# A Fourier mixing layer with a SoLU feed-forward behind it: where GpSimd's projection sums stand, and how the last two pairs are handled

## The chip, the cores and the metric

The kernel runs on one core of one Trainium2 chip. The core has five engines with an instruction queue each: TensorE (PE, matmuls; its weight loads are shown apart as PEld), VectorE (DVE), ScalarE (ACT), GpSimd (POOL) and SyncE (SP), which here issues transfers only. Each engine works through its own queue in order, and an instruction that waits holds up everything behind it on that engine. The metric is device time in microseconds (us).

## The reference

Eight sequences of 3136 tokens with 256 channels go through a Fourier filter, and every token then through a feed-forward block with a SoLU and a layer norm:

```
X = np.fft.rfft(x, axis=1)
y = np.fft.irfft(X * (filt_r + 1j * filt_i), n=3136, axis=1)
h = y.reshape(25088, 256) @ w_in                      # 1024 hidden
e = np.exp(h - h_max)
solu = h * e / (np.sum(e, axis=-1, keepdims=True) + 1e-09)
ln = (solu - mu) / np.sqrt(var + 1e-06) * g_ln
out = ln @ w_out                                      # 256 channels
```

## The kernel before

The 25088 tokens form 196 blocks of 128, and two blocks form a pair (98 pairs). One step of the main loop belongs to one block; there are 205 steps, written out by hand in `step(k)`, so the order of each engine's queue is the order of the calls there. `j` is `k // 2`. Both matrix products use a seven-product scheme for 2 x 2 blocks (as in Strassen's), so each needs sums of input blocks beforehand.

The way of a pair `q`, whose blocks are 2q and 2q+1:

- Steps 2q and 2q+1: `pair_sums` (four small sums s on GpSimd, one step ahead), seven `product` calls on TensorE, and `keep` and `finish` on ScalarE and VectorE, which give h and its running maximum.
- Two steps later for each block: `exponential` (ScalarE, into the single buffer e) and `normalize` (VectorE, L771). Three steps later: `turn` (a transpose of 32 x 32 blocks, VectorE, L787) and `square` (ScalarE, L779, which gives the variance).
- Two pairs make a group `g` of four blocks, which share one turned tile and one row of variances. Once the last block of the group is turned, `regroup` (eight transfers from SP, L799) puts a pair's tokens in order into two tiles solu_t: at step 2q+6. For the first pair of a group, `deviations` (GpSimd, L806 and L808, called rs below) computes the reciprocal deviations, SP writes them out as rows (L810), and `regroup_deviations` reads them back as rs_t (four transfers, L816).
- `project_sums(q, 0)` in odd step 2q+7 makes the sum u1 and the difference written over a part of solu_t; `project_sums(q, 1)` in even step 2q+8 makes u2 and u4. All four are GpSimd sums of 128 x 512 elements, and all are recorded under the helper's line L702. u2 and u4 have one buffer each, so a pair's u4 waits for the projection of the pair before that read it.
- Steps 2q+9 and 2q+10: seven `project` calls of four matmuls each (L844), in the order 1, 2, 6, 7, then 5, 3, 4. Products 1, 6, 5, 3 use one PSUM bank, and ScalarE's `keep_out` (L856, scaled by rs_t) must read it between any two of them. Products 2, 7, 4 use a second bank, read by `finish_out` on VectorE (L860). `store_out` writes the result from SP (L868).

The Fourier filter of sequence 2 to 8 runs along with this, at the steps that a hand-made plan gives: x rows are fetched, GpSimd makes a sum x (L260, in `products[k]`) and VectorE a difference, TensorE makes the first stage pa (L269), ScalarE evacuates it, GpSimd stores it (L280); a spectrum stage follows (pb, pc, g; filter rows f loaded by GpSimd, L642; g stored by GpSimd, L343), and the way back (rows t loaded by GpSimd, L356; py, join on VectorE). So GpSimd's queue holds sums, and issues of transfers, of both halves of the kernel. The plan ends before step 166; after that only the work on tokens is left. After step 195 nothing but the last blocks and projections remains (the tail, steps 196 to 204). Pool "r" holds four buffers of [128, 4, 256] for x and t rows; nothing uses them in the tail.

Of the kernel before, what the change touches and what calls it, by code (L numbers as in the profile page):

```python
# [9 lines left out]
FP32 = mybir.dt.float32  # L10
I32 = mybir.dt.int32
AFT = mybir.ActivationFunctionType
ALU = mybir.AluOpType
# [4 lines left out]
P = 128  # L18
B, S, C = 8, 3136, 256
DFF = 1024  # L20
# [9 lines left out]
NCH = 4  # L30
KD, KF = C // P, DFF // P
# [63 lines left out]
def kernel(  # L95
# [10 lines left out]
    nc = tc.nc  # L106
# [295 lines left out]
    with ExitStack() as st:  # L402
        fpool = pool("fp", 1, stack=st)
        pools = {name: pool(name + "0", bufs, stack=st)
                 for name, bufs in (("r", 1), ("t2", 1), ("p", 2), ("g", 2))}
# [152 lines left out]
        for n in range(16):  # L558
            (nc.sync, nc.scalar)[n % 2].dma_start(
                out=t2_0[NH * (n % 4):NH * (n % 4) + NH, n // 4, :], in_=rows_x[n:n + 1])  # L560
# [29 lines left out]
        for i0, n, rows in ((0, 4, P), (4, 4, P), (8, NP - 9, P), (NP - 1, 1, NQ)):  # L590
            f, at = filters[i0]
# [106 lines left out]
    def tokens(k, c):  # L698
        return y[:, c, P * (k % NT):P * (k % NT) + P]

    def sum_of(out, in0, in1, op):
        nc.gpsimd.tensor_tensor(out=out, in0=in0, in1=in1, op=op)  # L702

    def pair_sums(j):

# [29 lines left out]
    def finish(j, k, i, kept, bank):  # L735
# [10 lines left out]
        else:  # L746
            nc.vector.tensor_tensor_reduce(out=h_half(k, i), in0=ms[j, bank], in1=h_half(*kept),  # L747
                                           scale=1.0, scalar=sofar, op0=ALU.add, op1=ALU.min,
                                           accum_out=to)

    def exponential(k):

        e = wk.tile([P, DFF], FP32, name="e", tag="e")
        esum = small.tile([P, 1], FP32, name="esum", tag="esum", bufs=2)
        nc.scalar.activation(out=e, in_=hs[k], func=AFT.Exp, bias=nmaxs.pop(k)[:, 1:2], scale=-1.0,  # L755
                             accum_out=esum)
        es[k] = e, esum
# [17 lines left out]
    def square(k):  # L775

        g, i = divmod(k, 4)
        solu, nmu = solus.pop(k), squares.pop(k)
        nc.scalar.activation(out=solu, in_=solu, func=AFT.Square, bias=nmu, scale=-float(DFF),  # L779
                             accum_out=variances[g][:, i:i + 1])  # L780

    def turn(k):

        g, i = divmod(k, 4)
        if i == 0:
            turns[g] = wk2.tile([P, DFF // 32, 4, 32], FP32, name=f"turn_{g}", tag="turn")
        nc.vector.transpose(out=turns[g][:, :, i, :],  # L787
                            in_=solus[k].rearrange("p (f j) -> p f j", j=32))

    def regroup(p, i):  # L790


        g, second = divmod(p, 2)
        turned = turns[g].rearrange("p (k q) b i -> p k q (b i)", q=4)
        a = 2 * second + i
        st = upool.tile([P, KF, P], FP32, name=f"solu_t_{p}_{i}", tag=f"solu_t{i}")
        solu_ts[p, i] = st[:, 0:KF // 2, :], st[:, KF // 2:KF, :]
        for q in range(4):
            nc.sync.dma_start(out=st[32 * q:32 * q + 32, :, :],  # L799
                              in_=turned[32 * a:32 * a + 32, :, q, :])  # L800

    def deviations(p):
        g, second = divmod(p, 2)
        if not second:
            rs = small.tile([P, 4], FP32, name=f"rs_{g}", tag="rs", bufs=2)
            nc.gpsimd.tensor_scalar(out=rs, in0=variances.pop(g), scalar1=1.0 / DFF, scalar2=EPS_LN,  # L806
                                    op0=ALU.mult, op1=ALU.add)
            nc.gpsimd.tensor_tensor(out=rs, in0=rs, in1=neg_half, op=ALU.pow)  # L808
            rs_rows[g] = rows = rs_dram.tile([P, 4], FP32, name=f"rows_{g}", tag="rows")
            nc.sync.dma_start(out=rows, in_=rs)  # L810

    def regroup_deviations(g):
        rows = rs_rows.pop(g).rearrange("(a p) b -> b p a", p=32)
        rss[g] = small.tile([P, 4], FP32, name=f"rs_t_{g}", tag="rs_t")
        for b in range(4):
            nc.sync.dma_start(out=rss[g][32 * b:32 * b + 32, :], in_=rows[b])  # L816

    def project_sums(p, step):

        (a11, a12), (a21, a22) = solu_ts[p, 0], solu_ts[p, 1]  # L820
        if step == 0:
            s1 = upool.tile([P, KF // 2, P], FP32, name=f"u1_{p}", tag="u1")
            sum_of(s1, a21, a22, ALU.add)
            sum_of(a21, a11, a21, ALU.subtract)
            solu_sums[p] = s1, None, a21, None
        else:
            s2 = spool.tile([P, KF // 2, P], FP32, name=f"u2_{p}", tag="u2")
            s4 = spool.tile([P, KF // 2, P], FP32, name=f"u4_{p}", tag="u4")
            s1, _, s3, _ = solu_sums[p]
            sum_of(s2, s1, a11, ALU.subtract)  # L830
            sum_of(s4, a12, s2, ALU.subtract)
            solu_sums[p] = s1, s2, s3, s4

    def project(p, m):
# [19 lines left out]
    def keep_out(p, i, to):  # L854
        rs = out_half(p, i, 0)[1]
        nc.scalar.activation(out=out_half(p, *to)[0], in_=pos[p, 0], func=AFT.Copy, scale=rs)  # L856
# [6 lines left out]
    def store_out(p):  # L863
        g, second = divmod(p, 2)

        rows = out[4 * P * g:4 * P * g + 4 * P, :].rearrange("(b a i) c -> a b i c", a=4, i=32)
        for i in range(2):
            nc.sync.dma_start(out=rows[2 * second + i], in_=ots[p][:, i, :])  # L868
        del ots[p]
# [78 lines left out]
    def step(k):  # L948
        j, odd = divmod(k, 2)
        p = j - (LAG - 1) // 2 if odd else j - (LAG + 1) // 2  # L950
        if not 0 <= p < pairs:
            p = None
        hid, proj = k < blocks, p is not None
        for job in top[k] + stores[k] + products[k]:
            job()
        if odd and j + 1 < pairs:
            pair_sums(j + 1)
        if not odd:
            if hid:
                product(j, 1)  # L960
                keep(j, k, 0)
            if 2 <= k < blocks + 2:
                exponential(k - 2)
            if proj:
                project(p, 5)
                keep_out(p, 1, (0, 1))
            if hid:
                product(j, 2)
            if 3 <= k < blocks + 3:
                turn(k - 3)  # L970
            if hid:
                finish(j, k, 0, (k, 0), 1)
            if proj:
                finish_out(p, 1, 1, (0, 1), 1)
            for job in early[k]:
                job()
            if 3 <= k < blocks + 3:
                square(k - 3)
            if hid:
                product(j, 6)  # L980
                keep(j, k + 1, 0)
            if proj:
                project(p, 3)
                keep_out(p, 0, (0, 1))
                project(p, 4)
            for job in spectrum_loads[k]:
                job()
            if 0 <= j - 3 < pairs:
                regroup(j - 3, 0)
                regroup(j - 3, 1)  # L990
            if 0 <= j - 4 < pairs:
                project_sums(j - 4, 1)
            if 0 <= j - 3 < pairs:
                deviations(j - 3)
            if hid:
                product(j, 7)
            if 2 <= k < blocks + 2:
                normalize(k - 2)
            for job in second_parts[k] + middle[k] + first_parts[k]:
                job()  # L1000
            if proj:
                finish_out(p, 1, 0, (1, 0), 1)
                store_out(p)
        else:
            if hid:
                product(j, 5)
                keep(j, k - 1, 1)
                finish(j, k, 1, (k - 1, 1), 2)
            for job in early[k]:
                job()  # L1010
            if proj:
                project(p, 1)
                keep_out(p, 0, (0, 0))
                project(p, 2)
                finish_out(p, 0, 0, (0, 0), 1)
            if 2 <= k < blocks + 2:
                exponential(k - 2)
            if hid:
                product(j, 3)
                product(j, 4)  # L1020
            if 0 <= j - 3 < pairs:
                project_sums(j - 3, 0)
                if (j - 3) % 2 == 0:
                    regroup_deviations((j - 3) // 2)
            if proj:
                project(p, 6)
                project(p, 7)
            for job in second_parts[k] + middle[k]:
                job()
            if 3 <= k < blocks + 3:  # L1030
                turn(k - 3)
            if hid:
                finish(j, k - 1, 1, None, 0)
                finish(j, k, 0, (k, 0), 2)
            if 2 <= k < blocks + 2:
                normalize(k - 2)
            if proj:
                keep_out(p, 1, (1, 0))
            if 3 <= k < blocks + 3:
                square(k - 3)  # L1040
            for job in first_parts[k]:
                job()
        for job in late[k] + loads[k]:
            job()
        if k in (0, 1, 3, 4, 5, 6, 7):
            prepare_w_out(k - (k > 2))
# [37 lines left out]
```

## Time and profile before

| what | value |
|---|---|
| median of 3 runs | 1651.52 us (1638.6 to 1654.56) |
| the profiled execution's own time | 1631.78 us |
| its span, first to last instruction | 1630.0 us |
| mean granted TensorE clock | 0.986 |
| GpSimd, four projection sums per pair, 98 pairs each | mean 1352, 1453, 1508, 1621 ns |
| a pair's eight regroup transfers, issue on SP near the end | 5.36 us |
| share of time with a DMA engine busy, mean, from 1240 us on | 0.46 |

A page of the profile comes from one execution. Busy time is counted for each engine; a row in a timeline has the start, the length, the engine, the line, the operation with the tiles written and read, a count where equal rows were merged, and in square brackets the idle time of the engine just before and what ended it. A row of waits has the waiting engine, tile and line, then what was waited for, and the total in us, the number of times and the longest. A line in helper `sum_of` (L702) stands for all sums made through it; the tile names tell them apart.

### The profile page before, as it was taken

How to read it: one execution, taken by the hardware profiler on the slowest of the kernel's cores; microseconds unless marked ns; L12 is line 12 of the kernel's file. 1: busy time of each engine (PE TensorE's matmuls, PEld its weight loads, DVE VectorE, ACT ScalarE, POOL GpSimd, SP SyncE). 2: the span in 40 equal slices, each digit the busy share in tenths (PEclk: the TensorE clock that was granted, in tenths of full speed). 3: DMA queues.
4: the chain of work that ended last, by engine and by line, in shares of the span. 5: the costliest groups of instructions: out<-in, count | busy, mean ns of one | idle time of the engine just before them, and what ended most of it. 6: DMA issues, size and time to landing. Idle time of an engine off the chain costs nothing. (4 is left out here: it accounts for less than half of the span.)

```text
span 1630.0 us, 36971 instructions
## 1 busy us (share of the span) xinstructions
PE 1551.7 (95%) x12710; PEld 1048.3 (64%) x12710; DVE 1303.8 (80%) x2630; ACT 903.5 (55%) x1772; POOL 1151.2 (71%) x1328
## 2 busy tenths in 40 slices
PE   5898899999999999999999999999999999999997
PEld 1353366666666676667766676666766777777766
DVE  1686788898888889987889789887989777777772
ACT  2135455656655665565556655566555655566662
POOL 4446886588676867697687967778476666677774
PEclk8999899999999999999999999999999999999999
DMA  9887878777887768866787678866786555444443
GB/s 266 251 274 242 237 212 241 210 216 191 198 239 221 198 182 257 230 190 180 188 250 203 172 194 219 235 185 170 203 223 160 127 130 128 104 109 104 110 109 101
DMA packets 377805, 312.13 MB, mean 191 GB/s; under 512 B 63322, under 2 KB 343395, under 8 KB 377619
## 3 DMA queue, kind: packets, MB, share of 16 engines
q1 hardware_dynamic: 306260, 169.81, 40.8%
q0 software_dynamic: 34464, 101.68, 21.2%
q10 hardware_dynamic: 36896, 38.28, 7.9%
q8 instruction: 103, 1.69, 0.5%
q14 instruction: 82, 0.67, 0.1%
HBM read 124.86 MB, written 81.50 MB: 127 GB/s over the span
## 5 line engine op out<-in xcount | busy, mean ns | idle before, releaser
L844 PEld LDWEIGHTS o<-w_out_sb,solu_t 128*128 128x128 f32 x3136 | 382.0, 192 | 50.0 <-issue 43.6
L723 PE MATMUL m<-w_in_sb,s 128*128 128x512 f32 x784 | 398.7, 609 | 10.5 <-ACT h L733 5.3
L844 PE MATMUL o<-w_out_sb,solu_t 128*128 128x128 f32 x3136 | 401.5, 276 | 3.2 <-DVE ot L860 2.8
L844 PEld LDWEIGHTS o<-w_out_sb,u 128*128 128x128 f32 x2352 | 307.9, 192 | 147.4 <-issue 104.6
L702 POOL TENSOR_TENSOR u<-solu_t 128x512 f32<-128x512 f32 x98 | 132.5, 1352 | 276.6 <-DMA solu_t<-turn 165.8
L844 PE MATMUL o<-w_out_sb,u 128*128 128x128 f32 x2352 | 312.1, 276 | 8.7 <-ACT ot L856 7.8
L723 PE MATMUL m<-w_in_sb,y 128*128 128x512 f32 x588 | 311.1, 613 | 5.4 <-DVE nmax L747 3.3
L733 ACT COPY h<-m 128x512 f32<-128x512 f32 x294 | 173.2, 589 | 240.5 <-PE m L723 201.8
L771 DVE SCALAR_TENSOR_TENSOR h<-e,rsum,h 128x1024 f32<-128x1024 f32 x196 | 294.8, 1504 | 6.9
L856 ACT ACTIVATE ot<-o,rs_t 128x128 f32<-128x128 f32 x392 | 144.0, 367 | 254.1 <-PE o L844 238.3
L779 ACT ACTIVATE h<-h,nmu 128x1024 f32<-128x1024 f32 x196 | 224.9, 1148 | 59.6 <-DVE turn L787 59.2
L747 DVE CUSTOM_DVE_ANT_0 h<-m,h 128x512 f32<-128x512 f32 x196 | 134.0, 684 | 148.2 <-ACT h L733 94.8
L787 DVE STREAM_TRANSPOSE turn<-h 128x1024 f32<-128x1024 f32 x196 | 243.1, 1240 | 3.2
L755 ACT ACTIVATE e<-h,nmax 128x1024 f32<-128x1024 f32 x196 | 225.2, 1149 | 6.5 <-DVE h L771 6.5
L702 POOL TENSOR_TENSOR u<-solu_t,u 128x512 f32<-128x512 f32 x98 | 147.8, 1508 | 79.2 <-PE o L844 74.2
L723 PEld LDWEIGHTS m<-w_in_sb,s 128*128 128x128 f32 x784 | 128.6, 192 | 100.0 <-issue 85.6
L723 PEld LDWEIGHTS m<-w_in_sb,y 128*128 128x128 f32 x588 | 96.9, 192 | 104.4 <-issue 52.2
L860 DVE SCALAR_TENSOR_TENSOR ot<-o,rs_t,ot 128x128 f32<-128x128 f32 x294 | 102.0, 347 | 76.0 <-ACT ot L856 57.1
L702 POOL TENSOR_TENSOR u<-u,solu_t 128x512 f32<-128x512 f32 x98 | 158.9, 1621 | 1.2
L702 POOL TENSOR_TENSOR solu_t<-solu_t,solu_t 128x512 f32<-128x512 f32 x98 | 142.4, 1453 | 7.7
L702 POOL TENSOR_TENSOR s<-y 128x128 f32<-128x128 f32 x196 | 103.4, 527 | 0.4
L372 PEld LDWEIGHTS py<-wb_t,t 50*64 50x64 f32 x3584 | 57.6, 134 | 43.2 <-issue 21.2
(114 smaller groups left out, 1963.8 us busy)
## 6 DMA issues: line engine op xcount, KB each, us to landing
solu_t<-turn SPq DMA_DIRECT2D x784, 128.0 KB
out_dram<-ot SPq DMA_DIRECT2D x196, 128.0 KB
t<-d POOLq DMA_DIRECT2D x112, 200.0 KB, 4.4
d<-x POOLq DMA_DIRECT2D x100, 200.0 KB, 5.5
f<-f_dram POOLq DMA_DIRECT2D x39, 512.0 KB, 7.9
d<-g POOLq DMA_DIRECT2D x39, 512.0 KB, 5.5
t<-d ACTq DMA_DIRECT2D x36, 512.0 KB
x<-in_x_dram SPq DMA_DIRECT2D x112, 98.0 KB
```

The source lines that it names most:

```text
L372: nc.tensor.matmul(out=views[g][64 * h:64 * h + 64, cb, i, :], lhsT=t4[rows, i, c0:c0 + 64], rhs=wb_t[rows, 0:N1], start=True, stop=True)
L702: nc.gpsimd.tensor_tensor(out=out, in0=in0, in1=in1, op=op)
L723: nc.tensor.matmul(out=ms[j, bank], lhsT=lhsT, rhs=w_in_sb[:, w, :], start=m in (1, 2, 7), stop=True, skip_group_check=True)
L733: nc.scalar.copy(out=h_half(k, i), in_=ms[j, 0])
L747: nc.vector.tensor_tensor_reduce(out=h_half(k, i), in0=ms[j, bank], in1=h_half(*kept), scale=1.0, scalar=sofar, op0=ALU.add, op1=ALU.min, ...
L755: nc.scalar.activation(out=e, in_=hs[k], func=AFT.Exp, bias=nmaxs.pop(k)[:, 1:2], scale=-1.0, accum_out=esum)
L771: nc.vector.scalar_tensor_tensor(out=solu, in0=e, scalar=rsum, in1=solu, op0=ALU.mult, op1=ALU.mult, accum_out=nmu)
L779: nc.scalar.activation(out=solu, in_=solu, func=AFT.Square, bias=nmu, scale=-float(DFF), accum_out=variances[g][:, i:i + 1])
L787: nc.vector.transpose(out=turns[g][:, :, i, :], in_=solus[k].rearrange("p (f j) -> p f j", j=32))
L844: nc.tensor.matmul(out=pos[p, bank], lhsT=lhs[:, f, :], rhs=w[:, f, :], start=f == 0 and m in (1, 2, 7), stop=True, skip_group_check=True)
L856: nc.scalar.activation(out=out_half(p, *to)[0], in_=pos[p, 0], func=AFT.Copy, scale=rs)
L860: nc.vector.scalar_tensor_tensor(out=ot, in0=pos[p, bank], scalar=rs, in1=out_half(p, *kept)[0], op0=ALU.mult, op1=ALU.add)
```

## The change

Two edits. In the first, both halves of `project_sums` are called in the even step 2q+8: half 0 as the first thing in the step, half 1 where it was. `deviations` moves from the even step 2q+6 to the odd step 2q+7, and `regroup_deviations` from the odd step 2q+7 to the top of the even step 2q+8. In the second, the tail is rewritten: the exponentials of blocks 194 and 195 get buffers of pool "r" of their own, and both are made in step 196, as are both normalizations; blocks 194 and 195 are turned and squared in step 197; the last two pairs (96, 97) are regrouped there one after the other, pair 96 by SP and pair 97 by GpSimd's queue, three of the four tiles solu_t coming from pool "r"; and the sums of these two pairs are made by VectorE.

```diff
-    def sum_of(out, in0, in1, op):
-        nc.gpsimd.tensor_tensor(out=out, in0=in0, in1=in1, op=op)
+    def sum_of(out, in0, in1, op, engine=nc.gpsimd):
+        engine.tensor_tensor(out=out, in0=in0, in1=in1, op=op)
...
+    def spare_row(name):
+        return pools["r"].tile([P, NCH, C], FP32, name=name, tag="r")
+
     def exponential(k):
 
-        e = wk.tile([P, DFF], FP32, name="e", tag="e")
+        if k < blocks - 2:
+            e = wk.tile([P, DFF], FP32, name="e", tag="e")
+        else:
+            e = spare_row(f"e_{k}").rearrange("p i c -> p (i c)")
...
         a = 2 * second + i
-        st = upool.tile([P, KF, P], FP32, name=f"solu_t_{p}_{i}", tag=f"solu_t{i}")
+        if p == pairs - 1 or (p, i) == (pairs - 2, 1):
+            st = spare_row(f"solu_t_{p}_{i}").rearrange("p i c -> p (i c)").rearrange("p (n t) -> p n t", t=P)
+        else:
+            st = upool.tile([P, KF, P], FP32, name=f"solu_t_{p}_{i}", tag=f"solu_t{i}")
         solu_ts[p, i] = st[:, 0:KF // 2, :], st[:, KF // 2:KF, :]
+        dma = (nc.gpsimd if p == pairs - 1 else nc.sync).dma_start
         for q in range(4):
-            nc.sync.dma_start(out=st[32 * q:32 * q + 32, :, :],
+            dma(out=st[32 * q:32 * q + 32, :, :],
                               in_=turned[32 * a:32 * a + 32, :, q, :])
...
     def project_sums(p, step):
 
+        engine = nc.vector if p >= pairs - 2 else nc.gpsimd
...
+        last = blocks - 1
...
         hid, proj = k < blocks, p is not None
+        if not odd and 0 <= j - 4 < pairs:
+            if j % 2 == 0 and j - 4 < pairs - 2:
+                regroup_deviations((j - 4) // 2)
+            project_sums(j - 4, 0)
         for job in top[k] + stores[k] + products[k]:
             job()
...
+            if k == last + 1:
+                exponential(last)
             if hid:
                 product(j, 2)
-            if 3 <= k < blocks + 3:
+            if 3 <= k < blocks + 2:
                 turn(k - 3)
...
-            if 3 <= k < blocks + 3:
+            if 3 <= k < blocks + 2:
                 square(k - 3)
...
-            if 0 <= j - 3 < pairs:
+            if 0 <= j - 3 < pairs - 2:
                 regroup(j - 3, 0)
                 regroup(j - 3, 1)
             if 0 <= j - 4 < pairs:
                 project_sums(j - 4, 1)
-            if 0 <= j - 3 < pairs:
-                deviations(j - 3)
...
+            if k == last + 1:
+                normalize(last)
...
-            if 2 <= k < blocks + 2:
+            if 2 <= k < last + 2:
                 exponential(k - 2)
...
-            if 0 <= j - 3 < pairs:
-                project_sums(j - 3, 0)
-                if (j - 3) % 2 == 0:
-                    regroup_deviations((j - 3) // 2)
+            if 0 <= j - 3 < pairs - 2:
+                deviations(j - 3)
...
             if 3 <= k < blocks + 3:
                 turn(k - 3)
+            if k == last + 2:
+                turn(last)
...
-            if 2 <= k < blocks + 2:
+            if 2 <= k < last + 2:
                 normalize(k - 2)
...
             if 3 <= k < blocks + 3:
                 square(k - 3)
+            if k == last + 2:
+                square(last)
+                for q in (pairs - 2, pairs - 1):
+                    for i in range(2):
+                        regroup(q, i)
+                deviations(pairs - 2)
+                regroup_deviations((pairs - 2) // 2)
```

More of the change, by code (lines that the diff above doesn't have):

```diff
@@ L822, in project_sums @@
             s1 = upool.tile([P, KF // 2, P], FP32, name=f"u1_{p}", tag="u1")
-            sum_of(s1, a21, a22, ALU.add)
-            sum_of(a21, a11, a21, ALU.subtract)
+            sum_of(s1, a21, a22, ALU.add, engine)
+            sum_of(a21, a11, a21, ALU.subtract, engine)
             solu_sums[p] = s1, None, a21, None
@@ L829, in project_sums @@
             s1, _, s3, _ = solu_sums[p]
-            sum_of(s2, s1, a11, ALU.subtract)
-            sum_of(s4, a12, s2, ALU.subtract)
+            sum_of(s2, s1, a11, ALU.subtract, engine)
+            sum_of(s4, a12, s2, ALU.subtract, engine)
             solu_sums[p] = s1, s2, s3, s4
```

## The prediction

> **What bounds the kernel now.** I read the totals first, then busy time by stage, then TensorE's waits, then GpSimd's timeline in front of one of those waits, and last the end of the program. In the stage rows the columns are stretch, length, then busy time of PE, weight load, DVE, ACT and POOL.
>
> ```profile
> PE 1551.7 (95%) x12710; PEld 1048.3 (64%) x12710; DVE 1303.8 (80%) x2630; ACT 903.5 (55%) x1772; POOL 1151.2 (71%) x1328
> 200.00:1240.00 1040.00, 1018.25 (x9254) 694.97 (x9253) 900.72 (x1778) 608.04 (x1203) 777.52 (x910) 1.00 0.77 208
> 1240.00:1585.00 345.00, 344.86 (x2430) 248.98 (x2429) 267.32 (x593) 209.75 (x417) 239.84 (x260) 1.00 0.46 116
> 1585.00:1630.00 45.00, 30.67 (x256) 28.96 (x254) 13.73 (x31) 13.69 (x31) 21.74 (x17) 0.96 0.40 104
> ```
>
> TensorE sets the time. From 1240 to 1585, where only the token work runs, it never idles, so nothing can be won there. From 200 to 1240 it idles 1040.00 - 1018.25 = 21.8 us. From 1585 on it idles 14.3 us, of which about 6 lie after the last matmul (last store). The whole prize is thus about 30 us of 1630, plus a little before 200. Who holds TensorE up, and what does GpSimd wait for?
>
> ```profile
> PE pa L269 <- POOL x L260: 9.1, 6, 2.0
> POOL u L702 <- DMA solu_t<-turn: 165.8, 46, 9.1
> ```
>
> Six times (9.1 us, at most 2.0) the first-stage product pa waits for the sum x that GpSimd makes. GpSimd's own waits for solu_t are far longer, but they are idle time of an engine off the path. The timeline in front of one of the six, where TensorE stood still from 820.71 to 822.71:
>
> ```profile
> 810.51 1.85 POOL L702 TENSOR_TENSOR u<-solu_t 128x512 f32<-128x512 f32 x1 [6.78 <-DMA solu_t<-turn]
> 812.44 1.27 POOL L702 TENSOR_TENSOR solu_t<-solu_t,solu_t 128x512 f32<-128x512 f32 x1
> 813.65 1.09 POOL L356 DMA_DIRECT2D t<-d  x2
> 815.39 0.79 POOL L343 DMA_DIRECT2D d<-g  x1 [0.65 <-ACT h L733]
> 816.20 1.28 POOL L702 TENSOR_TENSOR u<-u,solu_t 128x512 f32<-128x512 f32 x1
> 817.56 1.27 POOL L702 TENSOR_TENSOR u<-solu_t,u 128x512 f32<-128x512 f32 x1
> 818.93 0.51 POOL L806 TENSOR_SCALAR rs<-var 128x4 f32<-128x4 f32 x1
> 819.52 1.04 POOL L808 TENSOR_TENSOR rs<-rs,neg_half 128x4 f32<-128x4 f32 x1
> 820.53 0.82 POOL L642 DMA_DIRECT2D f<-f_dram  x1
> 821.38 1.28 POOL L260 TENSOR_TENSOR x<-x 113x512 f32<-113x512 f32 x1
> ```
>
> The four u/solu_t sums stand in a row before x, held by the transfer solu_t; rs (deviations) stands between them and x. All six stalls (174.5, 354.3, 382.9, 479.1, 672.4, 822.7) come just after such an rs. In the tail, two stalls of TensorE belong to the last two pairs:
>
> ```profile
> 1610.43 1.13 PE L844 MATMUL o<-w_out_sb,u 128*128 128x128 f32 x8 [2.42 <-ACT ot L856]
> 1618.50 1.13 PE L844 MATMUL o<-w_out_sb,u 128*128 128x128 f32 x8 [0.80 <-POOL u L702]
> ```
>
> [...] two steps take 12.26 us in the full stage (1564.74 to 1577.00), which is 14 records of hidden products at 0.43 and 56 of projections at 0.111, the back-to-back spacings of the trace. [...] SP's eight transfers of one pair take 5.36 us to issue here; no trace of before shows two pairs at once. [...] this trace has 1.26 us for GpSimd undisturbed[...].
>
> **The change, part by part.** Written out queue by queue, TensorE's order is unchanged throughout, and VectorE's and ScalarE's up to step 195. So "moving" the first two sums from the odd step to the top of the next even step moves them past nothing but what GpSimd issues late in the odd step: the t<-d loads (two DMAs, 1.09), and f<-f_dram in a few early steps. No sum gets cheaper; solu_t still gates the same queue at the same place, and 165.8 us of waiting should stay mostly as it is. What shrinks is the queue between that gate and x.
>
> *Steady part.* rs (0.51 + 1.04 plus gaps, 1.6; 1.3 where undisturbed) goes behind x and the four s sums. The loads (1.09) go ahead of the gate, into idle time, where an odd step's load stood there. Stall by stall, the smaller of stall and relief: 174.5: 1.94 against 1.3; 354.3: 1.57 against 1.6; 382.9: 0.44 against 1.3; 479.1: 1.98 against 1.6 + 1.06; 672.4: 1.20 against 1.6 + 1.06; 822.7: 2.00 against 1.6 (the load's time turns into a longer wait for ScalarE before d<-g). Sum 1.3 + 1.57 + 0.44 + 1.98 + 1.20 + 1.6 = **-8.1 us**. Bounds: -3 if VectorE or ScalarE is late next, -11 with follow-on effects.
>
> *What the later rs costs.* SP now issues rows<-rs after the out stores and rs_t<-rows at the next even step, just before the second regroup. Before, from rs to the first ot that needs it there were 15.2 us at 820.6 and 11 to 16 in most groups; counted from the end of the s sums plus 1.6, the smallest is 5.6 (group 5: 357.0 to 364.2), typical 9. The chain needs 2.1 (rows, 1603.30) and 4.5 (rs_t issue to ot, 1605.45 to 1609.92) = 6.6, and TensorE has a projection and two products, 2.6 us, before that ot blocks it. It stalls only below 4.0: nowhere, so I take 0. SP's second regroup starts up to 2 us later, but its later half waits for a projection anyway. The cover is those 2.6 us.
>
> *Tail.* exponential(194) no longer waits for normalize(193) and exponential(195) follows it, but turn(195) stays behind normalize, two finish_outs and turn(194) on VectorE: from 1590.9 I add 0.35, 1.62, 0.35 (after the projection at 1592.7), 1.25 and 1.25, so it ends at about 1595.8 in place of 1597.34. Both squares now stand before project 5's keep_out, which costs TensorE about 0.8 in steps 198 and 199, inside the next wait. That wait is new: GpSimd issues pair 97's eight regroup DMAs and the rs **ahead of pair 95's four sums**. An issue of such a transfer on GpSimd is not shown: 0.51 (d<-x) to 0.79 (d<-g); I take 0.60, so 1595.8 + 4.8 + 1.3 (rs) + three sums at 1.27 and gaps, 4.0 = 1605.9 for the second u of pair 95, which TensorE used at 1600.81. Cost 5.1. Behind it the 2.42 goes (rs_t lands near 1608.6, its ot is due at 1605.9 + 5 x 0.89 + 0.72 = 1611) and the 0.80 goes, since both pairs have landed. Pairs 96's and 97's sums on VectorE, 8 x 0.69 = 5.5 (to 1.19 each by the pr row), fall into an engine with 13.7 us of work in 45, cost 0. Net 5.1 - 3.2 = **+1.9 us**, bounds -2 (turn and issues early) and +5 (0.79 an issue, two pairs sharing the DMA engines).
>
> Sum -8.1 + 1.9 = -6.2 us on the profiled execution's 1631.78, giving 1625.6. The median of the runs lies 19.7 above that execution, without a view that tells why; I carry the difference: 1651.52 - 6.2 = **1645**.
>
> **Rivals.** (1) *No change:* solu_t's landing, not the queue behind it, sets x, or the next matmul finds ScalarE late instead (2.27 at 243.85). For it: the gate waits stay. Against: rs before every stall. Only the tail's +1.9 is left: 1653. (2) *More is freed:* GpSimd's lateness also feeds the other 13.6 us of idle before 1240[...] (its sums stretch from 1.27 to 2.3 beside VectorE). All of that and no loss in the tail: -22, 1630. Against: those waits name ScalarE and VectorE. (3) *Slower:* the later rs. If in bursts of DMA SP's rs_t comes 4 us later than I count, ot blocks TensorE; at 0.7 us in the 33 groups of the mixed stage that is 23, less 6: 1668. It decides once rs to ot falls under 4.0 us. Against: ot waited for rs_t 4 times, 4.3 us in all, between 200 and 1585.
>
> **How the numbers follow.** Forecast 0.55 (own range 1641 to 1652), no change 0.20, more freed 0.12, slower 0.13. One per cent, 16.5 us, is about what a measurement of this kernel tells from no change: its three runs spread over 16. Below 1635 lies most of rival 2, above 1668 most of rival 3 and a failed tail: faster 0.12, same 0.76, slower 0.12. Range 1633 to 1660: forecast and no change with half the runs' spread, and part of the outer two.
>
> **What would show it.** After: pa's waits for x under 2 us in all; GpSimd's wait for solu_t still over 100; PE from 1240 to 1585 still full; the 2.42 gone, and a stall of some 4 us at pair 95's first u. Wrong if pa's stalls remain, if ot waits for rs_t by more than 15 us, or if pair 95 doesn't stall.

## The result, and the profile after

The changed kernel takes 1703.54 us (median of 4 runs, 1699.51 to 1711.76) against 1645.86 us (4 runs) before: a ratio of **1.0355, 95% interval 1.0281 to 1.0428**. The forecast was 1645 in a range from 1633 to 1660. The change makes the kernel about 58 us slower. The profiled execution spans 1700.0 us, 70 more than that of before, which was one of the faster of its kernel; its mean granted TensorE clock is 0.973 against 0.986.

In the changed kernel the lines have moved by some ten: projections are L855, `keep_out` L867, `finish_out` L871, rs L816 and L818, rows L820, rs_t L826, `regroup` L809, `store_out` L879, `turn` L793, hidden products still L723.

First the busy totals of the page of the changed kernel, then its stages (columns as in the prediction, the last three being the granted TensorE clock, the mean busy share of the DMA engines and what they moved in GB/s; the borders are moved so that the middle row is again the stage with token work alone):

```profile
PE 1571.7 (92%) x12710; PEld 1060.6 (62%) x12710; DVE 1300.3 (76%) x2638; ACT 904.5 (53%) x1772; POOL 1146.5 (67%) x1328
```

```profile
200.00:1305.00 1105.00, 1039.57 (x9297) 709.17 (x9296) 893.10 (x1788) 611.42 (x1209) 777.11 (x916) 0.98 0.73 198
1305.00:1650.00 345.00, 344.86 (x2430) 249.06 (x2429) 270.80 (x593) 210.31 (x417) 244.61 (x260) 1.00 0.47 117
1650.00:1700.00 50.00, 31.94 (x255) 30.31 (x254) 18.73 (x39) 13.44 (x31) 16.12 (x17) 0.94 0.36 92
```

The stage with token work alone is unchanged to the last digit: 344.86 us of TensorE in 345. The tail is 5 longer. The other 65 of the 70 us arise before it, in the stage where the Fourier filter runs along. There TensorE idles 1105.00 - 1039.57 = 65.4 us where it idled 21.8, and is busy for 1039.57 where it was busy for 1018.25, with about as many records (9297 and 9254). So 44 us are waits, and most of the other 21 are matmuls that run slower.

First waits of before that the prediction did not show, of the SP queue and of TensorE (waiting line, what was waited for, total us, times, longest), then those of the changed kernel:

```profile
SPq L799 <- DVE turn L787: 132.6, 36, 8.6
SPq L799 <- PE o L844: 99.9, 64, 3.8
...
SPq L816 <- DMA rows<-rs: 25.8, 19, 5.1
...
PE o L844 <- ACT ot L856: 7.8, 7, 2.4
PE m L723 <- ACT h L733: 5.3, 7, 2.3
PE m L723 <- DVE nmax L747: 3.3, 6, 0.8
```

```profile
SPq L826 <- DMA rows<-rs: 224.7, 49, 8.6
SPq L809 <- DVE turn L793: 76.3, 35, 5.5
SPq L809 <- PE o L855: 43.8, 51, 3.3
...
PE o L855 <- ACT ot L867: 28.9, 17, 4.4
PE m L723 <- ACT h L733: 21.4, 6, 7.8
PE m L723 <- DVE nmax L747: 11.6, 8, 3.2
...
ACT ot L867 <- DMA rs_t<-rows: 50.0, 17, 7.9
...
POOL u L702 <- DMA solu_t<-turn: 241.9, 48, 12.2
```

The new thing is the first row of the second list. SP, which before stood 19 times for the rows that it had just sent out, now stands for them in **every one of the 49 groups, 4.6 us each** (224.7 / 49). Everything queued behind the read-back on SP starts later: its regroups no longer wait long for turn and for the projections (76.3 and 43.8 where it was 132.6 and 99.9), which shows that SP is now the late one. GpSimd's wait for solu_t grows from 165.8 to 241.9. ScalarE waits 50.0 us for rs_t before it can read a projection out (ot). TensorE waits in three places that cost little before (28.9, 21.4 and 11.6 us where it was 7.8, 5.3 and 3.3), each behind another engine. That is 45 us more in all, about the 44 of the mixed stage.

One such place, in the timeline of the changed kernel:

```profile
1066.23 0.36 SPq L820 DMA_DIRECT2D rows<-rs  x1
...
1073.52 1.82 SPq L826 DMA_DIRECT2D rs_t<-rows  x4
1075.44 5.35 SPq L809 DMA_DIRECT2D solu_t<-turn  x8
1076.79 0.37 ACT L867 ACTIVATE ot<-o,rs_t 128x128 f32<-128x128 f32 x1 [7.54 <-DMA rs_t<-rows]
...
1077.30 2.05 PE L855 MATMUL o<-w_out_sb,u 128*128 128x128 f32 x8 [4.36 <-ACT ot L867]
```

SP sends rows at 1066.23 and cannot read them back before 1073.52: **7.3 us**, where the prediction counted 2.1 from the tail of before. Nothing goes out on SP in between (from 1066.6 to 1073.5). The regroup's eight issues then start at 1075.44.

The load of the Fourier filter isn't the only reason for the long landing, as SP's waits in the mixed stage (200 to 1305) and in the stage with token work alone (1305 to 1650) show:

```profile
SPq L826 <- DMA rows<-rs: 163.0, 33, 8.6
SPq L826 <- DMA rows<-rs: 53.3, 13, 5.8
```

That is 4.9 us each in the mixed stage, and still 4.1 where the DMA engines are no busier than before (0.47 against 0.46). In that second stage the kernel before sent the rows ahead of the stores of the result and could read them back after 2.05 us; the changed kernel sends them behind these stores, and takes 6.3 (first three rows: before, from 1329.05; last three: changed, from 1342.34):

```profile
1329.05 0.55 SPq L810 DMA_DIRECT2D rows<-rs  x1
1329.70 1.30 SPq L868 DMA_DIRECT2D out_dram<-ot  x2
1331.10 1.87 SPq L816 DMA_DIRECT2D rs_t<-rows  x4
...
1342.34 1.30 SPq L879 DMA_DIRECT2D out_dram<-ot  x2
1343.73 0.45 SPq L820 DMA_DIRECT2D rows<-rs  x1
1350.04 1.75 SPq L826 DMA_DIRECT2D rs_t<-rows  x4
```

The new place behind the stores thus goes with a slower landing; no run changes that place alone. And SP's standing costs TensorE nothing in this stage (344.86 of 345); the loss arises where the filter runs along.

The last line of the timeline further up (1077.30) shows the second cost: after the 4.36 us of standing, eight matmuls take 2.05 us, where eight of that kind take 1.06 in the tail of before. The granted clock of this trace stands at half there (0.50 from 1076.2 to 1083.0), and in the whole mixed stage in ten stretches: seven of 3.4 us, two of 6.8 and one of 10.2. The length of the stall alone doesn't tell which stall has half clock behind it. In the kernel before, one of 2.27 had, while the 2.42 in its tail, which the prediction shows, was followed by full speed (1.00 from 1610.4 to 1614.0). First row: the timeline behind the 2.27; second: the stretch there, with a clock of 0.50:

```profile
243.85 2.05 PE L723 MATMUL m<-w_in_sb,s 128*128 128x512 f32 x2 [2.27 <-ACT h L733]
243.60:247.00 3.40, 3.15 (x4) 1.51 (x5) 2.88 (x6) 1.50 (x4) 3.38 (x6) 0.50 0.94 309
```

In the mixed stage the clock stands at half for 47.8 us, in the kernel before for 10.2. As eight matmuls take about twice their time there (2.05 against 1.06), half of the difference, 19 us, is an estimate of what this adds: most of the 21.

### The profile page after: what moved, and what is told of

The parts are those of the page before. It is cut to its first block, busy times and chain, and to the rows that moved or that the text cites. A ratio compares the mean times of both kernels' runs of the same rounds, so it can differ in the third digit from the quotient of the medians.

```text
span 1700.0 us, 36989 instructions
## 1 busy us (share of the span) xinstructions
PE 1571.7 (92%) x12710; PEld 1060.6 (62%) x12710; DVE 1300.3 (76%) x2638; ACT 904.5 (53%) x1772; POOL 1146.5 (67%) x1328
## 5 line engine op out<-in xcount | busy, mean ns | idle before, releaser
L855 PEld LDWEIGHTS o<-w_out_sb,u 128*128 128x128 f32 x2352 | 312.7, 195 | 178.4 <-issue 122.9
L723 PE MATMUL m<-w_in_sb,s 128*128 128x512 f32 x784 | 398.3, 610 | 25.8 <-ACT h L733 21.4
L855 PEld LDWEIGHTS o<-w_out_sb,solu_t 128*128 128x128 f32 x3136 | 386.8, 194 | 49.9 <-issue 43.1
L855 PE MATMUL o<-w_out_sb,solu_t 128*128 128x128 f32 x3136 | 405.1, 278 | 4.7 <-DVE ot L871 4.2
L702 POOL TENSOR_TENSOR u<-solu_t 128x512 f32<-128x512 f32 x96 | 133.4, 1389 | 327.9 <-DMA solu_t<-turn 241.9
L855 PE MATMUL o<-w_out_sb,u 128*128 128x128 f32 x2352 | 319.3, 280 | 34.4 <-ACT ot L867 28.5
L723 PE MATMUL m<-w_in_sb,y 128*128 128x512 f32 x588 | 314.9, 619 | 16.0 <-DVE nmax L747 11.6
L867 ACT ACTIVATE ot<-o,rs_t 128x128 f32<-128x128 f32 x392 | 143.8, 367 | 304.6 <-PE o L855 216.1
L777 DVE SCALAR_TENSOR_TENSOR h<-e,rsum,h 128x1024 f32<-128x1024 f32 x196 | 298.5, 1523 | 6.9
L747 DVE CUSTOM_DVE_ANT_0 h<-m,h 128x512 f32<-128x512 f32 x196 | 133.9, 683 | 165.8 <-ACT h L733 117.7
L793 DVE STREAM_TRANSPOSE turn<-h 128x1024 f32<-128x1024 f32 x196 | 243.0, 1240 | 3.5 <-DVE ot L871 0.3
L761 ACT ACTIVATE e<-h,nmax 128x1024 f32<-128x1024 f32 x196 | 225.0, 1148 | 10.2 <-DVE h L777 10.0
L723 PEld LDWEIGHTS m<-w_in_sb,s 128*128 128x128 f32 x784 | 128.9, 192 | 113.9 <-issue 95.7
L871 DVE SCALAR_TENSOR_TENSOR ot<-o,rs_t,ot 128x128 f32<-128x128 f32 x294 | 101.9, 347 | 114.4 <-ACT ot L867 100.9
L723 PEld LDWEIGHTS m<-w_in_sb,y 128*128 128x128 f32 x588 | 97.8, 194 | 118.0 <-issue 50.1
L702 POOL TENSOR_TENSOR solu_t<-solu_t,solu_t 128x512 f32<-128x512 f32 x96 | 154.2, 1606 | 7.5
L702 POOL TENSOR_TENSOR u<-u,solu_t 128x512 f32<-128x512 f32 x96 | 145.9, 1520 | 0.9
L702 POOL TENSOR_TENSOR s<-y 128x128 f32<-128x128 f32 x196 | 95.4, 487 | 0.9 <-ACT y L398 0.5
```

Source lines behind the costliest of these rows:

```text
L702: engine.tensor_tensor(out=out, in0=in0, in1=in1, op=op)
L723: nc.tensor.matmul(out=ms[j, bank], lhsT=lhsT, rhs=w_in_sb[:, w, :], start=m in (1, 2, 7), stop=True, skip_group_check=True)
L777: nc.vector.scalar_tensor_tensor(out=solu, in0=e, scalar=rsum, in1=solu, op0=ALU.mult, op1=ALU.mult, accum_out=nmu)
L793: nc.vector.transpose(out=turns[g][:, :, i, :], in_=solus[k].rearrange("p (f j) -> p f j", j=32))
L855: nc.tensor.matmul(out=pos[p, bank], lhsT=lhs[:, f, :], rhs=w[:, f, :], start=f == 0 and m in (1, 2, 7), stop=True, skip_group_check=True)
L871: nc.vector.scalar_tensor_tensor(out=ot, in0=pos[p, bank], scalar=rs, in1=out_half(p, *kept)[0], op0=ALU.mult, op1=ALU.add)
```

## The experiments

Each ratio is to runs of the kernel before on the same chip; its 95% interval follows in brackets. "before" or "after" says what a kernel starts from; "after" is the changed kernel. Code is cut to the lines that matter.

### Which part of the change it is

Four kernels: the changed one with the deviations put back, and the three parts one at a time.

`e1_rs_back`, from after:

```diff
-            if j % 2 == 0 and j - 4 < pairs - 2:
-                regroup_deviations((j - 4) // 2)
...
+            if 0 <= j - 3 < pairs - 2:
+                deviations(j - 3)
...
-            if 0 <= j - 3 < pairs - 2:
-                deviations(j - 3)
+            if 0 <= j - 3 < pairs - 2 and (j - 3) % 2 == 0:
+                regroup_deviations((j - 3) // 2)
```

> The changed kernel, with deviations back in the even step and regroup_deviations back in the odd step; sums and tail stay changed. Theory W (SP stands waiting for rows<-rs before every rs_t, 224.7 us against 25.8 before, and that makes both rs_t and the second regroup late): the loss of the mixed stage goes, only the tail's 5 us stay, ratio to before 0.995 to 1.01. Rival S (the four sums together in the even step, or the loads ahead of them, cost the time): still slow, ratio 1.03 to 1.04. SP's wait for rows falls under 40 us by W.

Measured: 1636.34 us, 1.0006 (0.9973 to 1.0039). SP's wait for rows is 32.5 us in 18 places.

`e2_rs_alone`, from before, is the same edit the other way round: `deviations` to the odd step, `regroup_deviations` to the top of the next even step, nothing else.

> The kernel before, with only deviations moved to the odd step (ahead of the first sums) and regroup_deviations to the top of the next even step; sums and tail as before. Theory W: slow, ratio 1.03 to 1.05, SP's wait for rows near 225 us. Rival S: no loss, ratio 0.99 to 1.01.

Measured: 1691.66 us, 1.0369 (1.0297 to 1.0442). From its waits:

```profile
SPq L816 <- DMA rows<-rs: 207.9, 49, 7.7
...
PE o L844 <- ACT ot L856: 28.5, 18, 6.6
```

`e3_sums_alone`, from before: only `project_sums(q, 0)` moved to the top of the even step.

> The kernel before, with only the first two sums moved to the top of the next even step. Theory W: no loss, ratio 0.99 to 1.005 (GpSimd's queue loses only the late loads from behind the gate). Rival S: ratio 1.02 to 1.04.

Measured: 1634.83 us, 0.9979 (0.9958 to 1.0000).

`e4_tail_alone`, from before: only the tail's edits; the sums of the pairs up to 95 and all deviations stay where they were.

> The kernel before, with only the tail changed (two exponentials in step 196, last two pairs regrouped together, their sums on VectorE); pair 95's first two sums stay in the odd step. Both theories: the tail is 1 to 6 us longer or shorter, ratio 0.997 to 1.005; of the 65 us nothing comes from here.

Measured: 1640.86 us, 1.0013 (0.9995 to 1.0031).

What follows: the later deviations carry the whole loss. In us of some 1638 the three parts are +60, -3.4 and +2.1, which add up to 59; the whole change measured 58. The two small ones are not clear of no change: their intervals reach it.

### Which half of the deviations' move

`e5_rs_t_only`, from before: rs and rows stay early, only the read-back `regroup_deviations` moves to the top of the next even step.

> The kernel before, with only the reading back (rs_t) moved to the top of the next even step; rs and rows stay in the even step before. Theory W (the standing of SP for rows that were only just sent): rows have landed long before, SP's wait for rows under 10 us, no loss, ratio 0.99 to 1.01. Rival T (rs_t's own late place in SP's queue makes ot wait): slow, ratio over 1.02, ot waiting for rs_t by more than 40 us.

Measured: 1637.20 us, 1.0001 (0.9977 to 1.0025); SP waits for rows 26.9 us in 20 places, about as before, though under 10 was expected. A later read-back alone costs nothing: it is the later write, close ahead of the read-back, that makes SP stand.

`e7_rows_of_group_before`, as `e2_rs_alone`, but the read-back takes the rows of the group before, which have long landed. The outputs are thus scaled with another group's deviations.

```diff
-        rows = rs_rows.pop(g).rearrange("(a p) b -> b p a", p=32)
+        rows = rs_rows[max(g - 1, 0)].rearrange("(a p) b -> b p a", p=32)
```

> As the kernel in which rs alone is moved, but rs_t is read from the rows of the group before, so that it needn't wait for the rows just sent; every output is scaled by another group's deviations. Theory W: the loss goes, ratio 0.99 to 1.01. Rival G (rs done later on GpSimd, or rows and rs_t as such in front of the second regroup): ratio stays at 1.03 to 1.04.

Measured: 1653.27 us, 1.0085 (1.0025 to 1.0146), and hardly a wait for rows on SP (1.4 us). With every instruction in its late place but nothing to wait for, three quarters of the loss are gone. This wait is the cause of these three quarters; it has two effects, SP stands, and rs_t comes late to ot. The next runs part them.

`e8_rs_t_behind_regroup`, as `e2_rs_alone`, but the read-back is issued behind the eight transfers of the second regroup instead of ahead of them, so that the regroup doesn't stand behind it.

> As the kernel in which rs alone is moved, but rs_t is issued behind the second regroup of the even step, so that SP doesn't stand in front of that regroup. If the late regroup carries the loss (theory W, part b): ratio falls to 1.00 to 1.02. If ot's wait for rs_t carries it (part a): rs_t is some 5 us later still, ratio 1.05 or more.

Measured: 1858.11 us, 1.1358 (1.1304 to 1.1411). Its wait of TensorE:

```profile
PE o L844 <- ACT ot L856: 151.7, 49, 8.9
```

This trade is far worse. Some 5 us more for rs_t (eight issues) make ot late in all 49 groups: it had no spare left. This run thus says nothing about SP's standing.

### Which effect carries the loss

`e9_old_rs_t_for_ot`, as `e2_rs_alone`, but `keep_out` and `finish_out` scale with the rs_t of the group before; ot then never waits for the rs_t just read, and SP stands as it did.

```diff
-        return ots[p][:, i, P * n:P * n + P], rss[p // 2][:, ...]
+        return ots[p][:, i, P * n:P * n + P], rss[max(p // 2 - 1, 0)][:, ...]
```

> As the kernel in which rs alone is moved, but the outputs are scaled with the rs_t of the group before, which landed long ago; the transfers and SP's standing stay. If ot's wait carries the loss (part a): ratio falls to 0.99 to 1.01. If the late regroup carries it (part b): ratio stays over 1.02. Both shares show if it lies between.

Measured: 1697.63 us, 1.0377 (1.0282 to 1.0472). The theory that ot's wait is what costs falls. TensorE's waits for ot are down at 6.4 us, near the 7.8 of before; others stand in their place:

```profile
SPq L816 <- DMA rows<-rs: 218.6, 49, 7.7
...
PE m L723 <- ACT h L733: 29.1, 10, 7.0
...
ACT h L733 <- DMA rs_t<-rows: 35.1, 4, 10.3
ACT h L733 <- DMA t<-d: 35.0, 6, 8.7
```

ScalarE's copy of h doesn't use rs_t. The timeline of the same kernel shows one of the four copies that the trace has waiting for it all the same:

```profile
477.52 3.66 SPq L816 DMA_DIRECT2D rs_t<-rows  x4
477.58 0.40 ACTq L291 DMA_DIRECT2D t<-d  x1
...
483.95 0.37 ACTq L683 DMA_DIRECT2D de<-de_tbl  x1
...
484.35 0.59 ACT L733 COPY h<-m 128x512 f32<-128x512 f32 x1 [8.73 <-DMA rs_t<-rows]
...
485.08 2.05 PE L723 MATMUL m<-w_in_sb,s 128*128 128x512 f32 x2 [5.38 <-ACT h L733]
```

In front of the copy, on ScalarE's queue, stand two issues of transfers for the filter: t at 477.58 and, 6.0 us after the end of that, de at 483.95. The copy goes directly after de. The trace puts the end of ScalarE's 8.73 us of idle time down to the landing of a transfer of rs_t, which SP issued from 477.52 on. By what means a landing on SP's side holds an issue on ScalarE, no view shows; that de was what it held is read from the order alone. So a transfer that is late on SP goes with a late ScalarE, and through h with 5.38 us of standing on TensorE. The two matmuls behind that take 2.05 us, where two of that kind take 1.13 at 473.20 of the same trace.

Is this the route? Three kernels have the loop's fetches of t and de (L291, L683) issued by GpSimd instead of ScalarE:

```diff
-            dma = nc.sync.dma_start if e == 1 else nc.scalar.dma_start
+            dma = nc.sync.dma_start if e == 1 else nc.gpsimd.dma_start
...
-        nc.scalar.dma_start(out=de[:, 0:pairs],
+        nc.gpsimd.dma_start(out=de[:, 0:pairs],
```

`e10_old_rs_t_gpsimd_loads` is `e9_old_rs_t_for_ot` (outputs scaled with the group before's deviations) with this, `e11_rs_alone_gpsimd_loads` is `e2_rs_alone` with it, `e12_before_gpsimd_loads` is the kernel before with it, as a control.

> The kernel before with rs and rs_t at their new places, the outputs scaled with the group before's deviations (as in the run of that name), and the spectrum's fetches of the second and later stages (t from d, and de) issued by GpSimd instead of ScalarE, so that ScalarE issues no transfer in the loop. Theory: SP's standing reaches TensorE through ScalarE's queue: its issue of de is held until one of SP's transfers has landed, and the copies of h stand behind it. Then the wait of h for rs_t and t<-d (35.1 and 35.0 us) is gone, TensorE's wait for h falls from 28.3 to under 8 us, and the ratio from 1.038 to 1.005-1.018. Rival: the loss is SP's lateness itself (the regroups start later, u is late, and everything behind it): the waits only change their names, and the ratio stays at 1.03 or more. GpSimd pays some 92 issues of about 1 us for it, and stands for solu_t more; that could cost up to 1% by itself (the control, the kernel before with the same change of queue, says).

> As the run with rs and rs_t alone moved (1.037), with the outputs scaled rightly, and the spectrum's fetches of the second and later stages issued by GpSimd instead of ScalarE. Theory (ScalarE's queue carries SP's standing to TensorE): the waits of h for rs_t and for t<-d (26.7 and 16.8 us) go, but ot still waits for rs_t (52 us, of which TensorE stood 17.6), so about half of the loss stays: 1.012-1.025. Rival: 1.03 or more.

> The control: the kernel before with the spectrum's fetches of the second and later stages issued by GpSimd instead of ScalarE. If the change of queue costs and brings nothing by itself: 0.997-1.005. If GpSimd's issues delay its sums: up to 1.01.

Measured: 1689.87 us, 1.0312 (1.0255 to 1.0369); 1706.09 us, 1.0405 (1.0349 to 1.0461); control 1651.92 us, 1.0081 (1.0060 to 1.0101). The waits of h for rs_t and t<-d are gone in the first (none of them is as long as 3.6 us in total), and 1.0312 / 1.0081 = 1.023 still remains against its control. In the second VectorE's waits for ot grow instead, from 69.3 us in `e2_rs_alone` to 97.3 (both from 200 to 1585). The waits of `e10_old_rs_t_gpsimd_loads`:

```profile
PE m L723 <- DVE nmax L747: 32.6, 20, 4.6
PE o L844 <- POOL u L702: 25.4, 11, 5.2
...
DVE diff L254 <- DMA x<-in_x_dram: 62.5, 26, 6.0
```

With ScalarE free, VectorE stands 62.5 us for x rows, which SP fetches too, and the maxima (nmax) queued behind that are late; GpSimd's u is late with solu_t. My expectation was wrong: closing ScalarE's queue as a route does not bring the time back. What is late is SP, and each engine that needs something from it passes it on.

So the last test takes the standing away from SP. `e14_rs_alone_gpsimd_rows`, as `e2_rs_alone`, with both transfers of the deviations on GpSimd's queue; two sums lie between the write and the read-back there.

```diff
-            nc.sync.dma_start(out=rows, in_=rs)
+            nc.gpsimd.dma_start(out=rows, in_=rs)
...
-            nc.sync.dma_start(out=rss[g][32 * b:32 * b + 32, :], in_=rows[b])
+            nc.gpsimd.dma_start(out=rss[g][32 * b:32 * b + 32, :], in_=rows[b])
```

> As the run with rs and rs_t alone moved (1.037), with rows and rs_t issued by GpSimd instead of SP, at the same places in the program. Theory: the loss is SP's standing for rows (207.9 us there), which makes the regroups and the fetches of x behind it late. SP no longer waits for rows, its waits for turn go back towards 130 us, and the ratio falls to 0.998-1.012; GpSimd stands for rows in its place, with two sums (2.5 us) between the write and the read-back, some 2 us in 49 places. Rival: the loss is that rs_t itself is late (or GpSimd's standing is as dear as SP's): 1.025 or more.

Measured: 1675.98 us, 1.0206 (1.0161 to 1.0251), between both expectations. From its waits:

```profile
SPq L799 <- DVE turn L787: 239.6, 46, 13.5
...
PE o L844 <- ACT ot L856: 36.8, 16, 5.3
```

SP now has time to spare (239.6 us of waiting for turn), and much of what is left of the loss shows as ot's wait. `e17_old_rs_t_gpsimd_rows` takes that away as well (outputs scaled with the group before's deviations):

> rs and rs_t alone moved, rows and rs_t issued by GpSimd, and the outputs scaled with the deviations of the group before, so that neither SP stands for rows nor ot for its rs_t. If the loss has these two carriers and no third: 1.000-1.012, near the run with rows of the group before (1.0085). If rs's place on GpSimd or GpSimd's own standing is what is left: 1.015-1.021 as with rows on GpSimd alone.

Measured: 1658.42 us, 1.0117 (1.0075 to 1.0159), at the upper end of the first expectation.

Put together, rs late in all of them:

| SP stands for rows | ot waits for rs_t | kernel | ratio |
|---|---|---|---|
| yes | yes | `e2_rs_alone` | 1.037 |
| yes | no | `e9_old_rs_t_for_ot` | 1.038 |
| no | yes | `e14_rs_alone_gpsimd_rows` | 1.021 |
| no | no | `e17_old_rs_t_gpsimd_rows` | 1.012 |
| no | a little (18.7 us; 8.4 before) | `e7_rows_of_group_before` | 1.009 |

With SP's standing and no wait of ot, the loss is as large as with both. Taking the standing away as well is worth some 2.6% (`e9_old_rs_t_for_ot` to `e17_old_rs_t_gpsimd_rows`). ot's wait shows only when the standing is gone, and is then worth about 0.9%; the intervals of that pair just touch. They lie beside each other, so they don't add. About one per cent remains with neither. What it is (rs ahead of the sums on GpSimd, the place of the read-back among SP's issues, GpSimd's own standing in the one case) was not told apart.

### In the whole changed kernel, and a version without the loss

`e15_after_gpsimd_rows`: the changed kernel with the deviations' two transfers on GpSimd.

> The changed kernel (1.0355) with rows and rs_t issued by GpSimd instead of SP, at the same places in the program (the last group's too). Here no sums stand between rs and the read-back, so GpSimd stands longer, some 4 us in 49 places, and the sums behind it are later. Theory (SP's standing is what costs): 0.998-1.015. Rival: 1.025 or more.

Measured: 1696.38 us, 1.0334 (1.0294 to 1.0374): hardly a gain, the expectation was wrong. Its waits:

```profile
POOL rs_t L826 <- DMA rows<-rs: 180.0, 41, 7.3
...
PE o L855 <- POOL u L702: 35.8, 16, 9.0
```

Here no sums lie between the write and the read-back, so GpSimd stands 180.0 us in SP's place, and all four sums stand behind it. The standing is moved, not removed. The two sums that `e14_rs_alone_gpsimd_rows` has in between are the likely difference (its GpSimd stood 25.9 us between 200 and 1585); the two kernels differ in the place of the sums and in the tail too.

`e16_sums_alone_gpsimd_rows`: `e3_sums_alone` (rs early) with the two transfers on GpSimd.

> The kernel before with the first two sums alone moved (0.998), rs and rs_t at their places of before, rows and rs_t issued by GpSimd instead of SP. SP loses its 24 us of waits for rows; GpSimd stands for rows instead. Expected 0.993-1.000; if GpSimd's standing delays the sums, 1.000-1.006.

Measured: 1636.74 us, 0.9971 (0.9951 to 0.9991). It takes 0.3% less than the kernel before; that is no more than `e3_sums_alone` within the intervals, so nothing is shown for the change of queue itself.

`e13_rs_back_mended_tail`: `e1_rs_back` with pair 97's regroup issued by GpSimd one step later, behind pair 95's sums.

> The changed kernel with rs and rs_t at the places of the kernel before (1.0006 by itself), and the last pair's eight issues put behind pair 95's sums on GpSimd's queue instead of ahead of them. The stalls of 4.8 us for pair 95's second u and 1.7 behind it go, pair 97's tiles land some 5 us later, with pair 96's projections (about 7 us) ahead of them. Expected 0.995-0.999; if the last pair's tiles then come late, or the tail's stalls return elsewhere, 1.000.

Measured: 1637.85 us, 0.9989 (0.9963 to 1.0014). The stall for pair 95's second u shrinks from 4.77 to 1.04 us, but one of 7.26 us comes up behind ot in the last pairs, which the trace puts down to a store of the result. The tail's time is moved, not won.

## Why the prediction was wrong

**What bounds the kernel:** right. TensorE sets the time, the stage with token work alone stayed full (344.86 of 345), and what happened lies in the mixed stage and the tail.

**Steady part, -8.1:** right in what happens to the queue. pa's waits for x fell from 9.1 to 1.7 us, below the 2 that was named, and solu_t's gate stayed above 100. The moved sums alone bring them to 2.5 (`e3_sums_alone`), rs's exit alone to 1.8 (`e2_rs_alone`). Whether that is time won is not clear: `e3_sums_alone` measured -3.4 us (0 to -7), and rs's exit could not be had without the loss. One reading was wrong: ahead of the stall at 174.5, rs had ended at 166.0, six us before x began, so it was not what made that x late.

**Tail, +1.9:** right in size, though no change lies within the interval too. `e4_tail_alone` measured +2.1 (-0.8 to +5.1). In the changed kernel:

```profile
1660.42 4.75 POOL L809 DMA_DIRECT2D solu_t<-turn  x8 [4.19 <-DVE turn L793]
...
1670.40 2.08 PE L855 MATMUL o<-w_out_sb,u 128*128 128x128 f32 x8 [4.79 <-POOL u L702]
1670.46 0.56 SPq L820 DMA_DIRECT2D rows<-rs  x1
...
1681.25 0.37 ACT L867 ACTIVATE ot<-o,rs_t 128x128 f32<-128x128 f32 x1 [4.35 <-DMA out_dram<-ot]
1681.67 1.16 PE L855 MATMUL o<-w_out_sb,u 128*128 128x128 f32 x8 [2.50 <-ACT ot L867]
```

An issue on GpSimd costs 4.75 / 8 = 0.59 us (0.60 taken), the stall for pair 95 is 4.79 us (5.1), and the eight sums on VectorE take 0.68 to 0.69 us each (0.69, which the four sums of this size in L673 show before: 688 ns). The 2.42 did not go: a stall of 2.50 for ot stands in its place. The trace puts that ot down to a store of the result, which stands on SP behind the rows and their read-back; rows leaves only at 1670.46, behind pair 96's issues. The half clock after the 4.79 (0.50 from 1670.1 to 1673.4, 2.08 us for eight matmuls) was not counted. These lie in the tail's 5 us of this execution, the upper bound that was kept.

**"What the later rs costs ... nowhere, so I take 0":** this is the step that failed, by 60 us (`e2_rs_alone`). Three terms of it were wrong:

- The landing of rows, 2.1 us, was read at 1603.30, where the filter is done and rows goes out ahead of the stores. The prediction noted that it would go out behind them, and gave that no price. In the mixed stage SP waits 4.9 us in the mean, and in the example above the chain from rows to ot takes 10.6 us (1066.23 to 1076.79), where 6.6 were counted.
- SP's standing was priced at "up to 2 us later", with the regroup's later half hidden behind a projection. It stands in 49 of 49 groups, and in the mixed stage what is behind it on SP (regroups, x rows) and beside it (ScalarE's own issues) has no such cover. SP did wait long for turn and for projections before (132.6 and 99.9), but that time to spare did not lie at the place of the read-back.
- The cover of 2.6 us at ot was held to be enough. In `e2_rs_alone` TensorE stood 28.5 us for ot in 18 places, and in `e8_rs_t_behind_regroup`, with some 5 us more, at all 49.

**Rival 3** named the right edit and, with 23 us, too small a price. Its sign to look for, ot waiting for rs_t by more than 15 us, came (50.0), but it is not what decides: without that wait the loss is the same (`e9_old_rs_t_for_ot`). The mechanism that decides, a queue standing for its own write, was in none of the rivals.

**The base:** the forecast carried 19.7 us between the profiled execution and the median of three runs. That difference did not last: with a fourth run the median of before is 1645.86, and 47 runs beside the first experiments have 1638.49. So the forecast of 1645 for a gain of 6 lies where the kernel before already was.

## What to carry to other kernels

When a write to HBM and its read-back share a queue, price the stretch between them as standing time of that queue, with a landing time read in the stage with the same load and at the same place in the queue, and ask what is queued behind. Either keep enough other work of that queue between the two (the kernel before had the stores there) or leave both where they are: moving a cheap operation later moved its transfers too, and these cost 60 us where the whole steady part was to save 8. If one wait is taken away and the time stays, look for what is late in common, as here SP behind ot, h, nmax and u.

## What the runs showed of the hardware that was not expected

- A write of 128 x 4 values to HBM took 7.3 us in the mixed stage (`after`, 1066.23 to 1073.52) until its read-back could be issued, against 2.1 us in the tail of before. Sent behind the stores of the result, it kept SP waiting 4.1 us in the mean even with the DMA engines only 0.47 busy.
- A stall cost TensorE more than its own length where the granted clock stood at 0.50 behind it: eight matmuls took 2.05 to 2.08 us instead of 1.06 (`after`, 1077.30 and 1670.40), and the stretches at 0.50 in the mixed stage were 3.4 to 10.2 us long. A stall of 2.27 us was once followed by one. In the mixed stage this adds an estimated 19 us (half of 47.8 - 10.2) to 44 us of extra waits.
- ScalarE's copy of h, which doesn't read rs_t, waited 8.73 us, by the trace until a transfer of rs_t from SP had landed; ScalarE's issue of an unrelated transfer (483.95) stands directly in front of it (`e9_old_rs_t_for_ot`). With these issues on GpSimd's queue the waits of h for rs_t (35.1 us) and for t<-d (35.0 us) were each under 3.6 us in total (`e10_old_rs_t_gpsimd_loads`). By what means the two are tied was not shown.
